# A router's first expert layer: three blocks of tokens by 15 part products, with the operands' sums moved between engines

## The chip, the cores and the metric

The kernel runs on one core of one Trainium2 chip. The metric is the device time of one execution in microseconds (us). Its engines are TensorE (PE, with PEld for its weight loads), VectorE (DVE), ScalarE (ACT), GpSimd (POOL) and SyncE (SP, which here only issues transfers). All data is float32.

## The reference, cut to what matters

A gated linear attention makes 3072 tokens of 384 values; a cosine router sends each token to one of eight experts, and the expert's two layers make the output.

```python
state = alpha_t * state + k_t (x) v_t;  y_t = q_t @ state      # 4 batches, 8 heads, 768 steps, 48 values a head
x = y as 3072 tokens x 384
xn = x / (norm(x) + 1e-6);  en = expert_emb / (norm(expert_emb) + 1e-6)
logits = xn @ en.T / tau                                        # 8 experts
expert_idx = argmax(logits);  gate = softmax(logits)[expert_idx]
for e in range(8):                                              # w1: 384 x 1024, w2: 1024 x 384
    h = relu(x[expert_idx == e] @ w1[e])
    out[expert_idx == e] = gate * (h @ w2[e])
```

## The kernel before, in words

The attention runs until about 155 us and nothing in it changes. Tokens are sorted by expert in DRAM as they are routed. Then `run(i)` goes over the eight experts. An expert has three blocks of 128 tokens (`NC`); of expert 0 two were done before (`EARLY`), and its single block takes the plain `first_layer`. What is more than three blocks of an expert goes through `half_block` of 64 rows, behind a branch in `run_extra`; in the profiled execution it ran three times. The weights of expert i + 2 are fetched while expert i runs.

**First layer of three blocks** (`first_layer_pair`, matmuls at L999). Hidden units are taken in four pairs of 128-wide tiles (f and f + 4). For each pair the 2 x 3 tiles of w1 and the tokens, in two halves of 192, are multiplied in the manner of Strassen: 11 products of 192 columns in place of 12, in four PSUM banks (`pq0` to `pq3`). Their left sides are tiles of w1 or the sums s1 to s4 and `dif` (`w1_m`), the right sides tokens or the sums t1 to t4 (`xT_m`). ScalarE copies a bank out (L1010) and does the ReLU (L1007); VectorE adds (`add`, by `by_dve`, so recorded at L922).

**Sums of the operands.** `mix_first(i + 1)` makes the next expert's five sums of w1 (128x512) and four of tokens (128x192) on VectorE (L976), after the first layer of expert i. `mix_weights` makes four sums of w2 as eight operations of 128x384 on GpSimd (L946), at the start of the expert that uses them. `mix_hidden` makes four sums of the hidden values on VectorE, in two parts, put as `fill` between the adds of the last two pairs and behind them.

**Second layer.** The third block goes through `second_layer`: eight matmuls of 384 columns (L906), evicted by VectorE with the gate (L909). Blocks 0 and 1 go through `second_layer_pair`: seven products of four matmuls of 192 columns (L1047), in four banks. ScalarE writes u0, u1 (L1061, L1062) and half of y0 (L1069), and VectorE collects the rest (`gated`, L1054). GpSimd scatters each block's output to its token rows with an indirect DMA (L817).

**Next expert's preparation.** `prepare` transposes a block of the next expert's tokens on TensorE (L842) after each pair of tiles, and VectorE copies it to xT. `prepare_gates` (L850 to L877) makes the next expert's gates: squares and square root on ScalarE (L857, L858), the largest logit and differences on VectorE (L870 to L873, `gsh`), Exp on ScalarE (L874), sum and reciprocal on VectorE.

**What sets the order.** Each engine runs its instructions in one order, which a scheduler sets when the kernel is built; `turn_of` and `issue_after` fix parts of it. TensorE's products follow the list `pe`, and VectorE's adds the list `dve`; `done_pair` holds the last work of a pair, behind which the next expert's branch and GpSimd's sums stand. Between two experts all engines read the branch's condition (L1165).

```python
def by_dve(call, *args):
    with turn_of(dve):
        dve[:] = [call(*args)]
    return dve[0]
...
hT = hp.tile([P, FT, NC * P], FP32, name="hT")[:, :, 0:n]
```

Of the kernel before, what the change touches and what calls it, by code (L numbers as in the profile page):

```python
# [27 lines left out]
def kernel(  # L28
# [756 lines left out]
    with ExitStack() as c3:  # L785
# [15 lines left out]
        w1_m = wp.tile([P, 5, F // 2], FP32, name="w1_m")  # L801
        xT_m = xp.tile([P, 4, NC * P // 2], FP32, name="xT_m")
# [34 lines left out]
        def turn(xg, xT, n, by=None):  # L837

            px = ps_x.tile([P, KT, P], FP32, name="pxg")
            with turn_of(pe if by else []):  # L840
                for k in range(KT):
                    done = nc.tensor.transpose(  # L842
                        px[:, k, 0:n], xg[0:n, k * P : (k + 1) * P], ident[0:n, 0:n]
                    )
            if by is None:
                return nc.vector.tensor_copy(xT, px[:, :, 0:n])
            pe[:] = [done]
            return by(nc.vector.tensor_copy, xT, px[:, :, 0:n])
# [51 lines left out]
        def second_layer(w2_t, hT, gate, col):  # L900

            py = ps_y.tile([P, DM], FP32, name="pyo")
            y = yp.tile([P, DM], FP32, name="y")
            with pe_turn():
                for f in range(FT):
                    pe[:] = [nc.tensor.matmul(  # L906
                        py, lhsT=hT[:, f], rhs=w2_t[:, f], start=(f == 0), stop=(f == FT - 1),
                    )]
            nc.vector.tensor_scalar(y, py, gate, None, ALU.mult)  # L909
            with turn_of(drained):  # L910
                return scatter(y, col)
# [6 lines left out]
        fill = []  # L918
# [5 lines left out]

        def filled(n):
            for _ in range(min(n, len(fill))):
                fill.pop(0)()
# [8 lines left out]
        def mix_weights(w2_t, j):  # L936
# [3 lines left out]
            to, x, y = ((t1, b12, b11), (t2, b22, t1), (t4, b21, t2), (t3, b22, b12))[j]  # L940

            n = FT // 4
            with turn_of(done_pair):
                for k in range(2):
                    f = slice(k * n, k * n + n)
                    nc.gpsimd.tensor_tensor(to[:, f], x[:, f], y[:, f], ALU.subtract)  # L946

        def mix_hidden(hT, f0, f1):

            a11, a12, a21, a22 = (  # L950
                hT[:, j * FT // 2 + f0 : j * FT // 2 + f1, i * P : i * P + P]
                for i in range(2) for j in range(2)
            )
            s1, s2, s3, s4 = (hT_m[:, k, f0:f1] for k in range(4))
            for to, x, y, op in (
                (s1, a21, a22, ALU.add), (s2, s1, a11, ALU.subtract),
                (s4, a12, s2, ALU.subtract), (s3, a11, a21, ALU.subtract),
            ):
                yield lambda to=to, x=x, y=y, op=op: by_dve(nc.vector.tensor_tensor, to, x, y, op)

        def mix_first(i):

            w1_t, xT = w1_s[i % NW], xT_s[i % 2]
            a11, a12, a21, a22 = quarters_w1(w1_t, 0, F // 2)
            m = NC * P // 2
            (b11, b12), (b21, b22) = ((xT[:, k, 0:m], xT[:, k, m : 2 * m]) for k in range(2))
            s1, s2, s3, s4, dif = (w1_m[:, k] for k in range(5))
            t1, t2, t3, t4 = (xT_m[:, k] for k in range(4))
            for to, x, y, op in (
                (s1, a21, a22, ALU.add), (s2, s1, a11, ALU.subtract),  # L970
                (s3, a11, a21, ALU.subtract), (s4, a12, s2, ALU.subtract),
                (dif, w1_t[:, 2, 0 : F // 2], w1_t[:, 2, F // 2 : F], ALU.subtract),
                (t1, b12, b11, ALU.subtract), (t2, b22, t1, ALU.subtract),
                (t3, b22, b12, ALU.subtract), (t4, b21, t2, ALU.subtract),
            ):
                nc.vector.tensor_tensor(to, x, y, op)  # L976

        def quarters_w1(w1_t, c0, c1):
            return [w1_t[:, k, j * F // 2 + c0 : j * F // 2 + c1] for j in range(2) for k in range(2)]

        def first_layer_pair(w1_t, hT, xT, f):

            cut = slice(f * P, f * P + P)
            a11, a12, a21, a22 = quarters_w1(w1_t, f * P, f * P + P)
            m = NC * P // 2
            r1, r2 = slice(0, m), slice(m, 2 * m)
            s1, s2, s3, s4, dif = (w1_m[:, k, cut] for k in range(5))  # L990
            t1, t2, t3, t4 = (xT_m[:, k] for k in range(4))
            c1, c2 = w1_t[:, 2, cut], w1_t[:, 2, F // 2 + f * P : F // 2 + f * P + P]
            a, b, c, d = (bank(j)[:, 0:m] for j in range(4))
            u1, u2, u3 = (yp.tile([P, m], FP32, name=f"v{j}", bufs=2) for j in range(3))
            h1, h2 = hT[:, f], hT[:, FT // 2 + f]

            def product(to, left, right, start, stop):
                with pe_turn():
                    pe[:] = [nc.tensor.matmul(  # L999
                        to, lhsT=left, rhs=right, start=start, stop=stop, skip_group_check=True,  # L1000
                    )]

            def add(to, p, u):
                by_dve(nc.vector.tensor_tensor, to, p, u, ALU.add)

            def relu(h, p):
                return nc.scalar.activation(h, p, AF.Relu)  # L1007

            product(a, a11, xT[:, 0, r1], True, False)
            nc.scalar.copy(u1, a)  # L1010
            product(b, s2, t2, True, True)
            add(u2, b, u1)
            product(c, s3, t3, True, False)
            add(u3, c, u2)
            filled(1)
            product(d, c2, xT[:, 2, r2], True, False)
            product(d, s1, t1, False, False)
            add(h2[:, r2], d, u3)
            filled(1)
            product(a, a12, xT[:, 1, r1], False, False)  # L1020
            product(a, c1, xT[:, 2, r1], False, True)
            relu(h1[:, r1], a)
            product(c, a22, t4, False, False)
            product(c, c2, xT[:, 2, r1], False, True)
            add(h2[:, r1], c, u2)
            relu(h2, h2)
            product(d, s4, xT[:, 1, r2], False, False)
            product(d, dif, xT[:, 2, r2], False, True)
            add(h1[:, r2], d, u2)
            filled(2)  # L1030
            return relu(h1[:, r2], h1[:, r2])
        def second_layer_pair(w2_t, hT, gate, col):
# [5 lines left out]
            a11, a12, a22 = hT[:, 0:n, 0:P], hT[:, n:FT, 0:P], hT[:, n:FT, P : 2 * P]  # L1038
            a, b, c, d = (bank(j)[:, 0:m] for j in range(4))
            y0 = yp.tile([P, DM], FP32, name="y")  # L1040
            y1 = yp.tile([P, DM], FP32, name="y")
            g0, g1 = gate[:, 0:1], gate[:, 1:2]
# [15 lines left out]

            u = yp.tile([P, 5, m], FP32, name="u", bufs=1)
            product(a, a11, b11, True, False)  # L1060
            nc.scalar.mul(u[:, 0], a, g0)  # L1061
            nc.scalar.mul(u[:, 1], a, g1)  # L1062
            product(b, s2, t2, True, True)
            gated(u[:, 2], b, g0, u[:, 0])
            gated(u[:, 3], b, g1, u[:, 1])
            product(c, s3, t3, True, False)
            gated(u[:, 4], c, g1, u[:, 3])
            product(a, a12, b21, False, True)
            nc.scalar.mul(y0[:, 0:m], a, g0)  # L1069
            product(d, s1, t1, True, False)  # L1070
            gated(y1[:, m:DM], d, g1, u[:, 4])
            product(c, a22, t4, False, True)
            gated(y1[:, 0:m], c, g1, u[:, 3])
            scatter(y1, col[:, 1:2])
            product(d, s4, b22, False, True)
            done_pair[:] = pe[0], gated(y0[:, m:DM], d, g0, u[:, 2])
            done_pair.append(scatter(y0, col[:, 0:1]))
# [33 lines left out]
        def run(i):  # L1111
# [5 lines left out]
            hT = hp.tile([P, FT, NC * P], FP32, name="hT")[:, :, 0:n]  # L1117
            pair = blocks_run(i) == NC
            dve[:] = [] if pair else ready
            if pair:  # L1120
                for j in range(4):
                    mix_weights(w2_t, j)
                for f in range(FT // 2):
                    done = first_layer_pair(w1_t, hT, xT, f)
                    if f < len(nxt):
                        turned = prepare(i + 1, f, by_dve)

                    if f >= FT // 4:
                        f0 = 2 * (f - FT // 4)
                        fill.extend(mix_hidden(hT, f0, f0 + 2))  # L1130
                filled(len(fill))
# [5 lines left out]
            if nxt:  # L1137
                with turn_of(dve):
                    mix_first(i + 1)
# [8 lines left out]
            for t in range(2 if pair else 0, blocks_run(i)):  # L1148
                sent = second_layer(
                    w2_t, hT[:, :, t * P : (t + 1) * P], gate[:, t : t + 1], col[:, t : t + 1]  # L1150
# [67 lines left out]
        gates(exg[:, 0:EARLY], egt[:, 0:EARLY], esx[:, 0:EARLY], EARLY)  # L1218
# [8 lines left out]

        for i in range(E):
# [37 lines left out]
```

## Time and profile before

| | |
|---|---|
| three runs | 417.14, 415.33, 417.24 us, median 417.14 |
| profiled execution | 415.06 us; span from first to last instruction 413.3 us |
| granted TensorE clock, mean | 0.994 |
| VectorE, ScalarE, GpSimd busy | 267.8, 178.4, 190.9 us |
| first layer, products of three blocks (L999) | 280 passes on plain tiles, 168 on two sums, and smaller groups |
| VectorE's adds of a bank into hidden values (L922) | 84 of 128x192, 357 ns each |
| GpSimd's w2 sums (L946) | 56 of 128x384, 998 and 996 ns each |

An execution of the program is recorded by the hardware profiler; the page gives each engine's busy time, the chain of work that ended last, and groups of instructions with count, busy time and mean length. A timeline row reads: start in us, length in us, engine, line of the code, operation, output <- inputs, shape, and how many instructions in a row it holds; in brackets the idle time ahead and what ended it. Matmuls are pipelined, so rows that follow each other overlap a little; the pace is read from start to start. One fp32 matmul is two passes of the array, and each pass has a record of its own.

### The profile page before, as it was taken

The numbers are of one execution on the slowest core, as the hardware profiler recorded it, in microseconds if no ns is written. First come the engines' busy times: TensorE is split into PE (matmuls) and PEld (weight loads), VectorE is DVE, ScalarE is ACT, GpSimd is POOL, SyncE is SP. The second block draws the span as 40 slices with busy tenths as digits, with TensorE's granted clock in tenths as the row PEclk, the third lists the DMA queues.
The fourth block names the chain that finished last, engine by engine and source line by source line (L and its number), as shares of the span: only waits on it lengthen the run. The fifth ranks groups of instructions, "written<-read, shape, count | busy, mean of one in ns | idle before, by whom it ended". The sixth has DMA issues, their size and how long they took to land. (4 is left out here: it accounts for less than half of the span.)

```text
span 413.3 us, 11425 instructions
## 1 busy us (share of the span) xinstructions
PE 403.6 (98%) x4346; PEld 358.6 (87%) x4346; DVE 267.8 (65%) x725; ACT 178.4 (43%) x430; POOL 190.9 (46%) x283
## 2 busy tenths in 40 slices
PE   6999999999999999999999999999999999999994
PEld 6888999899889886879799799799989979979974
DVE  6899788788898334715855845943672694593541
ACT  4555554555455435453523523522451352452410
POOL 7446787777766547308018028024301802702701
PEclk9999999999999999999999999999999999999999
DMA  9999999999998944959009219117303801001001
GB/s 137 160 162 157 159 214 172 199 182 205 194 185 257 387 172 143 293 186 365 6 18 321 92 39 329 56 38 272 121 19 105 302 2 38 22 0 53 3 17 43
DMA packets 119374, 60.20 MB, mean 146 GB/s; under 512 B 102287, under 2 KB 113816, under 8 KB 119312
## 3 DMA queue, kind: packets, MB, share of 16 engines
q1 hardware_dynamic: 115208, 49.14, 51.0%
q0 software_dynamic: 3728, 10.16, 7.1%
q8 instruction: 41, 0.67, 0.8%
q14 instruction: 21, 0.17, 0.1%
q10 hardware_dynamic: 376, 0.05, 0.1%
HBM read 49.69 MB, written 11.45 MB: 148 GB/s over the span
## 5 line engine op out<-in xcount | busy, mean ns | idle before, releaser
L817 POOL DMA_INDIRECT out_dram<-y,sx x25 | 24.4, 977 | 158.1 <-DVE gsh L873 77.6
L999 PE MATMUL pq<-xT,w 128*128 128x192 f32 x280 | 64.5, 328 | 0.6
L922 DVE TENSOR_TENSOR hT<-pq,v 128x192 f32<-128x192 f32 x84 | 30.0, 357 | 32.8 <-PE pq L999 30.8
L999 PEld LDWEIGHTS pq<-xT,w 128*128 128x128 f32 x280 | 47.3, 190 | 2.8 <-DVEq L1165 1.7
L507 POOL TENSOR_TENSOR qs<-qc,a 128x512 f32<-128x512 f32 x24 | 30.6, 1275 | 33.9 <-DVE a L503 23.4
L906 PE MATMUL pyo<-w,hT 128*128 128x384 f32 x128 | 43.3, 492 | 0.0
L906 PEld LDWEIGHTS pyo<-w,hT 128*128 128x128 f32 x128 | 23.7, 190 | 15.3
L999 PE MATMUL pq<-xT_m,w_m 128*128 128x192 f32 x168 | 36.5, 326 | 0.0
L1007 ACT ACTIVATE hT<-hT 128x384 f32<-128x384 f32 (+1 forms) x56 | 24.8, 443 | 23.1 <-DVE hT L922 19.9
L479 DVE TENSOR_TENSOR_SCAN r<-pa,inr 128x511 f32<-128x511 f32 x24 | 29.2, 1216 | 6.3 <-PE pa L194 4.4
L503 DVE TENSOR_TENSOR_SCAN a<-pa,ini 128x512 f32<-128x512 f32 x24 | 29.3, 1223 | 1.1
L1047 PE MATMUL pq<-w_m,hT_m 128*128 128x192 f32 x168 | 29.6, 326 | 0.0
L946 POOL TENSOR_TENSOR w_m<-w 128x384 f32<-128x384 f32 x28 | 27.4, 998 | 3.5 <-DMA out_dram<-y,sx 2.7
L999 PEld LDWEIGHTS pq<-xT_m,w_m 128*128 128x128 f32 x168 | 28.9, 190 | 0.0
L313 POOL DMA_INDIRECT xs<-x,dest x24 | 24.3, 1012 | 9.5 <-issue 4.5
L1007 ACT ACTIVATE hT<-pq 128x192 f32<-128x192 f32 x28 | 9.2, 330 | 43.5 <-PE pq L999 43.5
L1047 PEld LDWEIGHTS pq<-w_m,hT_m 128*128 128x128 f32 x168 | 27.7, 190 | 0.0
L946 POOL TENSOR_TENSOR w_m<-w,w_m 128x384 f32<-128x384 f32 x28 | 27.1, 996 | 0.0
L191 PE MATMUL sc<-qs,kr 64*64 64x128 f32 x768 | 26.5, 276 | 0.0
L191 PE MATMUL pyx<-sm,vt 128*64 128x128 f32 x384 | 26.3, 279 | 0.0
L922 DVE TENSOR_TENSOR v<-pq,v 128x192 f32<-128x192 f32 x56 | 20.0, 356 | 9.1 <-ACT v L1010 4.4
L1054 DVE SCALAR_TENSOR_TENSOR y<-pq,gt,u 128x192 f32<-128x192 f32 x21 | 8.8, 418 | 24.6 <-PE pq L1047 24.6
(199 smaller groups left out, 896.5 us busy)
## 6 DMA issues: line engine op xcount, KB each, us to landing
w<-in_moe_w_dram SPq DMA_DIRECT2D x16, 1536.0 KB, 9.2
kt<-in_k_dram SPq DMA_DIRECT2D x24, 192.0 KB, 4.3
qt<-in_q_dram SPq DMA_DIRECT2D x24, 192.0 KB, 4.5
vt<-in_v_dram SPq DMA_DIRECT2D x24, 192.0 KB, 5.8
xg<-xs SPq DMA_DIRECT2D x22, 196.5 KB, 7.7
at<-in_alpha_dram SPq DMA_DIRECT2D x24, 168.0 KB, 5.0
xg<-xs SPq DMA_DIRECT2D x8, 98.2 KB
at<-in_alpha_dram SPq DMA_DIRECT2D x24, 22.5 KB, 4.2
```

The source lines that it names most:

```text
L191: last["pe"] = nc.tensor.matmul(*args, **kwargs)
L313: ins = nc.gpsimd.indirect_dma_start(out=xs, out_offset=bass.IndirectOffsetOnAxis(ap=rows, axis=0), in_=x, in_offset=None, bounds_check=E ...
L479: nc.vector.tensor_tensor_scan(r[:, L - 2 :: -1], pa[:, L - 1 : 0 : -1], inr[:, L - 2 :: -1], 1.0, ALU.mult, ALU.add,)
L503: d["a_scan"] = by_dve = nc.vector.tensor_tensor_scan(a, pa, ini, 0.0, ALU.mult, ALU.add)
L507: by_pool = nc.gpsimd.tensor_tensor(qs.rearrange("p n t -> p (n t)"), d["qc"], a, ALU.mult)
L817: ins = nc.gpsimd.indirect_dma_start(out=out, out_offset=bass.IndirectOffsetOnAxis(ap=col, axis=0), in_=y, in_offset=None, bounds_check=N - 1,
L906: pe[:] = [nc.tensor.matmul(py, lhsT=hT[:, f], rhs=w2_t[:, f], start=(f == 0), stop=(f == FT - 1),)]
L922: dve[:] = [call(*args)]
L946: nc.gpsimd.tensor_tensor(to[:, f], x[:, f], y[:, f], ALU.subtract)
L999: pe[:] = [nc.tensor.matmul(to, lhsT=left, rhs=right, start=start, stop=stop, skip_group_check=True,)]
L1007: return nc.scalar.activation(h, p, AF.Relu)
L1047: pe[:] = [nc.tensor.matmul(to, lhsT=left[:, f], rhs=right[:, f], start=start and f == 0, stop=stop and f == n - 1, skip_group_check=True,)]
```

## The change

The first layer now takes an expert's three blocks at once (`first_layer_blocks`): a product's left side is four tiles of w1 side by side or of its sums (128x512), its right side one block of 128 tokens or a sum of blocks; 15 products of four matmuls make the 2 x 3 outputs, each of 128x512 in one bank. A bank is read on its way (copied by ScalarE or added by VectorE into the hidden values in place) and accumulated on by later products. `between` puts the next expert's transposes after products 3, 6, 9 and 14, and ScalarE copies them. There are ten sums of w1, made by GpSimd one expert ahead (those of expert 1 by VectorE, after the gates of the blocks that were done early), and the sums of blocks by VectorE, in 13 operations of 128x128 or 128x256. The four sums of w2 move to VectorE, as four operations of 128x768. The hidden sums are four operations of 128x512 after the first layer. The third block's output is evicted by ScalarE. The pair's second layer collects s-products and a22's in bank a, which is read by ScalarE or VectorE and accumulated on four times; y0 is scattered before y1. The hidden values have one buffer in place of two.

In the order that the scheduler sets, ScalarE's u0 (L1093 after) stands behind the Exp of the next expert's gates (L872 after), where u0 and u1 stood ahead of it; and VectorE's w2 sums for an expert stand in the second layer of the expert before it, t1 and t2 ahead of the gated y1, t3 and t4 behind it and on either side of the last gated y0.

Removed functions are in the code above; of the new ones all lines are shown.

```diff
-        w1_m = wp.tile([P, 5, F // 2], FP32, name="w1_m")
-        xT_m = xp.tile([P, 4, NC * P // 2], FP32, name="xT_m")
+        w1_m = wp.tile([P, 10, F // 2], FP32, name="w1_m")
+        xT_m = xp.tile([P, 16, P], FP32, name="xT_m")
...
-            return by(nc.vector.tensor_copy, xT, px[:, :, 0:n])
+            return by(xT, px[:, :, 0:n])
...
-            nc.vector.tensor_scalar(y, py, gate, None, ALU.mult)
+            by(y, py, gate)
...
-        def mix_weights(w2_t, j):
+        def mix_weights(w2_t):
             (b11, b12), (b21, b22) = quarters(w2_t)
             t1, t2, t3, t4 = (w2_m[:, k] for k in range(4))
-            to, x, y = ((t1, b12, b11), (t2, b22, t1), (t4, b21, t2), (t3, b22, b12))[j]
...
-                    nc.gpsimd.tensor_tensor(to[:, f], x[:, f], y[:, f], ALU.subtract)
+            for to, x, y in ((t1, b12, b11), (t2, b22, t1), (t3, b22, b12), (t4, b21, t2)):
+                by_dve(nc.vector.tensor_tensor, to, x, y, ALU.subtract)
...
+        def hidden(hT, t):
+            return [hT[:, j * FT // 2 : (j + 1) * FT // 2, t * P : (t + 1) * P] for j in range(2)]
+        def mix_hidden(hT):
+            (a11, a12), (a21, a22) = (hidden(hT, t) for t in range(2))
+            s1, s2, s3, s4 = (hT_m[:, k] for k in range(4))
             for to, x, y, op in (
+                (s3, a11, a21, ALU.subtract), (s1, a21, a22, ALU.add),
+                (s2, s1, a11, ALU.subtract), (s4, a12, s2, ALU.subtract),
             ):
+                by_dve(nc.vector.tensor_tensor, to, x, y, op)
...
+        def mix_first_weights(i, by):
+            (a11, a12, a13), (a21, a22, a23) = halves_w1(w1_s[i % NW])
+            g, g2, e, f2, q9, q7, q10, k6, q13, k = (w1_m[:, j] for j in range(10))
             for to, x, y, op in (
+                (g, a11, a12, ALU.add), (g2, g, a22, ALU.subtract), (e, a12, a13, ALU.subtract),
+                (f2, e, a22, ALU.subtract), (q9, a21, g2, ALU.subtract),
+                (q7, a23, q9, ALU.subtract), (q10, g, q7, ALU.subtract),
+                (k, f2, a23, ALU.add), (k6, k, a21, ALU.subtract),
+                (q13, q7, a13, ALU.subtract),
             ):
+                by(to, x, y, op)
...
+        def mix_first_rows(i):
+            xT, m = xT_s[i % 2], xT_m
+            b1, b2, b3 = (xT[:, k, 0 : NC * P].rearrange("p (t n) -> p t n", n=P) for k in range(KT))
+            y1, z1, y2, z2, x5, x12, x10, x6, x1, x4, x7, x13, s, x15, x11, x14 = (
+                m[:, j : j + 1] for j in range(16)
+            )
+            v = nc.vector
+            def one(b, t):
+                return b[:, t : t + 1]
+            v.tensor_tensor(m[:, 0:2], b2[:, 1:3], b3[:, 1:3], ALU.add)
+            v.tensor_tensor(y2, one(b2, 0), one(b1, 0), ALU.subtract)
+            v.tensor_tensor(x1, y1, y2, ALU.add)
+            v.tensor_tensor(x11, y2, one(b3, 0), ALU.add)
+            v.tensor_tensor(m[:, 4:6], b1[:, 0:2], y1.to_broadcast([P, 2, P]), ALU.subtract)
+            v.scalar_tensor_tensor(
+                out=x4, in0=y2, scalar=-1.0, in1=one(b3, 1), op0=ALU.mult, op1=ALU.subtract
+            )
+            v.tensor_tensor(x7, z1, one(b1, 0), ALU.subtract)
+            v.tensor_tensor(s, one(b2, 2), one(b3, 1), ALU.add)
+            v.tensor_tensor(m[:, 6:8], s.to_broadcast([P, 2, P]), b1[:, 0:3:2], ALU.subtract)
+            v.tensor_tensor(x13, one(b1, 2), z1, ALU.subtract)
+            v.tensor_tensor(z2, one(b1, 2), one(b2, 2), ALU.subtract)
+            v.tensor_tensor(x14, one(b3, 0), x7, ALU.subtract)
+            v.tensor_tensor(x15, one(b1, 1), x6, ALU.add)
...
+        def first_layer_blocks(w1_t, hT, between):
+            (a11, a12, a13), (a21, a22, a23) = halves_w1(w1_t)
+            g, g2, e, f2, q9, q7, q10, k6, q13, k = (w1_m[:, j] for j in range(10))
+            y1, z1, y2, z2, x5, x12, x10, x6, x1, x4, x7, x13, _, x15, x11, x14 = (
+                xT_m[:, j] for j in range(16)
+            )
+            (c11, c21), (c12, c22), (c13, c23) = (hidden(hT, t) for t in range(NC))
+            n = FT // 2
+            def grid(j):
+                return bank(j)[:, 0 : n * P].rearrange("p (f t) -> p f t", t=P)
+            A, B, C, D = (grid(j) for j in (2, 1, 3, 0))
             def product(to, left, right, start, stop):
                 with pe_turn():
+                    for f in range(n):
+                        pe[:] = [nc.tensor.matmul(
+                            to[:, f], lhsT=left[:, f * P : (f + 1) * P], rhs=right,
+                            start=start and f == 0, stop=stop, skip_group_check=True,
+                        )]
+            def add(c, p):
+                by_dve(nc.vector.tensor_tensor, c, p, c, ALU.add)
+            def relu(c, p):
+                return nc.scalar.activation(c, p, AF.Relu)
+            product(A, a22, x1, True, False)
+            nc.scalar.copy(c21, A)
+            product(B, g2, y1, True, False)
+            nc.scalar.copy(c12, B)
+            product(D, a13, x11, True, True)
+            nc.scalar.copy(c11, D)
+            between()
+            product(A, f2, y2, False, False)
+            add(c11, A)
+            product(B, g, x5, False, False)
+            add(c11, B)
+            relu(c11, c11)
+            D = grid(0)
+            product(D, a11, x12, True, True)
+            add(c12, D)
+            between()
+            product(A, e, x4, False, False)
+            add(c12, A)
+            relu(c12, c12)
+            product(B, q7, x7, False, False)
+            nc.scalar.copy(c13, B)
+            product(C, q10, x10, True, False)
+            nc.scalar.copy(c23, C)
+            between()
+            product(A, k6, x6, False, False)
+            add(c13, A)
+            product(B, q9, z1, False, False)
+            add(c23, B)
+            product(C, q13, x13, False, True)
+            add(c13, C)
+            relu(c13, c13)
+            product(A, k, z2, False, False)
+            add(c23, A)
+            relu(c23, c23)
+            product(B, a23, x14, False, True)
+            add(c21, B)
+            relu(c21, c21)
+            between()
+            product(A, a21, x15, False, True)
+            return relu(c22, A)
...
+            a, b, d = (bank(j)[:, 0:m] for j in (0, 1, 3))
+            u = yp.tile([P, 3, m], FP32, name="u", bufs=1)
...
             product(a, a11, b11, True, False)
             nc.scalar.mul(u[:, 0], a, g0)
-            nc.scalar.mul(u[:, 1], a, g1)
-            product(b, s2, t2, True, True)
-            gated(u[:, 2], b, g0, u[:, 0])
-            gated(u[:, 3], b, g1, u[:, 1])
-            product(c, s3, t3, True, False)
-            gated(u[:, 4], c, g1, u[:, 3])
-            product(a, a12, b21, False, True)
-            nc.scalar.mul(y0[:, 0:m], a, g0)
+            product(b, a12, b21, True, True)
+            gated(y0[:, 0:m], b, g0, u[:, 0])
+            product(a, s2, t2, False, False)
+            nc.scalar.mul(u[:, 1], a, g0)
             product(d, s1, t1, True, False)
-            gated(y1[:, m:DM], d, g1, u[:, 4])
-            product(c, a22, t4, False, True)
-            gated(y1[:, 0:m], c, g1, u[:, 3])
-            scatter(y1, col[:, 1:2])
+            nc.scalar.mul(u[:, 2], d, g1)
+            product(a, s3, t3, False, False)
+            gated(y1[:, m:DM], a, g1, u[:, 2])
             product(d, s4, b22, False, True)
-            done_pair[:] = pe[0], gated(y0[:, m:DM], d, g0, u[:, 2])
-            done_pair.append(scatter(y0, col[:, 0:1]))
+            gated(y0[:, m:DM], d, g0, u[:, 1])
+            scatter(y0, col[:, 0:1])
+            product(a, a22, t4, False, True)
+            done_pair[:] = pe[0], nc.scalar.mul(y1[:, 0:m], a, g1)
+            done_pair.append(scatter(y1, col[:, 1:2]))
...
-            hT = hp.tile([P, FT, NC * P], FP32, name="hT")[:, :, 0:n]
+            hT = hp.tile([P, FT, NC * P], FP32, name="hT", bufs=1)[:, :, 0:n]
...
             if pair:
-                for j in range(4):
-                    mix_weights(w2_t, j)
-                for f in range(FT // 2):
-                    done = first_layer_pair(w1_t, hT, xT, f)
-                    if f < len(nxt):
-                        turned = prepare(i + 1, f, by_dve)
-                    if f >= FT // 4:
-                        f0 = 2 * (f - FT // 4)
-                        fill.extend(mix_hidden(hT, f0, f0 + 2))
-                filled(len(fill))
+                mix_weights(w2_t)
+                left = list(range(len(nxt)))
+                rest = []
+                def between():
+                    if left:
+                        rest[:] = [prepare(i + 1, left.pop(0), nc.scalar.copy)]
+                done = first_layer_blocks(w1_t, hT, between)
+                if nxt:
+                    turned = rest[0]
+                mix_hidden(hT)
...
             if nxt:
+                if pair:
+                    mix_first_weights(i + 1, nc.gpsimd.tensor_tensor)
                 with turn_of(dve):
-                    mix_first(i + 1)
+                    mix_first_rows(i + 1)
...
                 sent = second_layer(
-                    w2_t, hT[:, :, t * P : (t + 1) * P], gate[:, t : t + 1], col[:, t : t + 1]
+                    w2_t, hT[:, :, t * P : (t + 1) * P], gate[:, t : t + 1], col[:, t : t + 1],
+                    nc.scalar.mul if pair else nc.vector.tensor_scalar_mul,
                 )
...
-        gates(exg[:, 0:EARLY], egt[:, 0:EARLY], esx[:, 0:EARLY], EARLY)
+        known = gates(exg[:, 0:EARLY], egt[:, 0:EARLY], esx[:, 0:EARLY], EARLY)
...
+        with turn_of([known]):
+            mix_first_weights(1, nc.vector.tensor_tensor)
```

## The prediction

> **What bounds the kernel now.** I read the busy table, then the chain that ended last, then TensorE's timeline for one expert, and at last what the other engines do in that expert's second half.
>
> ```profile
> PE 403.6 (98%) x4346; PEld 358.6 (87%) x4346; DVE 267.8 (65%) x725; ACT 178.4 (43%) x430; POOL 190.9 (46%) x283
> ...
> PE 7%; POOL 0%; issue 0%; POOLq 0%; DVE 0%
> PE pq L999 3%; PE pq L1047 2%; PE pyo L906 1%; POOL out_dram L817 0%; POOLq L1161 0%; DVE y L1054 0%
> ```
>
> TensorE is busy for 98% of the span, and the chain ends in its products: the first layer (L999), the second layer of the pair (L1047) and of the third block (L906). VectorE has a third of its time free and GpSimd half. So fewer TensorE passes are worth their whole time, and work on VectorE, ScalarE or GpSimd costs nothing until TensorE must wait for it. TensorE waits for them at few places, so one late result shows at once.
>
> **The gain on TensorE.** An expert's first layer is now 4 x 11 products; each is one fp32 matmul, which the trace records as two passes, so 88 passes of 192 columns. After, it is 15 x 4 matmuls, 120 passes of 128 columns. The timeline of TensorE has rows for both widths:
>
> ```profile
> 167.93 1.50 PE L894 MATMUL pq<-xT,w 128*128 128x128 f32 x12
> 169.27 0.49 PE L842 MATMUL pxg<-ident,xg 128*128 128x128 f32 x3
> ...
> 303.45 1.46 PE L1047 MATMUL pq<-w,hT 128*128 128x192 f32 x8
> 304.75 2.76 PE L1047 MATMUL pq<-w_m,hT_m 128*128 128x192 f32 x16
> ```
>
> From start to start, eight passes of 192 columns take 1.30 us (162.5 ns each), and twelve of 128, each with weights of its own, take 1.34 us (111.7 ns each). So 88 x 162.4 ns = 14.29 us becomes 120 x 111.7 ns = 13.40 us: 0.89 us less, times the seven experts with three blocks = **-6.2 us**. The columns fall by an eleventh (15,360 for 16,896), and a column of the narrow pass costs 0.873 ns for 0.846; the gain is what is left. The second layer keeps its 16 + 56 passes.
>
> The Trainium skill ("TensorE: Matmul & The Clock Gate", Back-to-back issue gap) speaks against narrow products: 81 ns for a matmul of 128 columns and 131 ns for one of 512, much more per column. By an estimate from that page, a straight line between the two, 192 columns take 89 ns, and the change would cost TensorE some 13 us over the seven experts in place of saving 6. The rows above do not agree (111.7 and 162.4 ns), and they decide.
>
> **Handovers inside the first layer.** A bank is written by a product, read by ScalarE (copy of 128x512, 0.59 us at L489) or VectorE (add with one operand in PSUM, 0.69 us at L486), and accumulated on three products later. A product takes 8 x 0.1117 = 0.89 us, so two products, 1.79 us, lie between; the way out of TensorE is some 0.3 us (a pass's latency and its semaphore), so bank and reader need about 1.0 us. Slack 0.6 us or more; only the last product has less, and in the last expert, without a transpose in front of it, I charge **+0.2 us** once. The gap of 0.3 us at the branch between experts stays. Copies of xT go to ScalarE, which is busy for 43%: nothing.
>
> **The start.** Expert 1's ten w1 sums go to VectorE, 10 x 0.60 us = 6.0 us where 5 x 0.60 + 1.3 were. They may stand in front of a copy of xT near 172.6 us. Between nothing (VectorE's free third) and 1.2 us (two such sums), I take **+0.5 us**.
>
> **w2's sums on VectorE.** Four of 128x768, about 0.95 us each (estimate from 0.68 for 512 and 0.42 for 256 columns), during the second layer. They stand in VectorE's queue ahead of the gated y1 (L1088), which the last product waits for, since it accumulates in the same bank. From the end of the fourth product the queue needs t1 + t2 + y1 = 0.95 + 0.95 + 0.42 + 0.4 of latency = 2.7 us, and the fifth and sixth products cover 2.6. I take 0.15 us each, x 6 = **+0.9 us** (bounds 0 and 0.4 each).
>
> **One bank for the collection.** Before, product 3 of the pair writes a bank of its own. After, it accumulates into bank a, so it must wait until ScalarE's u0 (L1093) has read a. In ScalarE's queue u0 stands behind the Exp of the next expert's gates. Exp needs gsh, which VectorE computes after the hidden sums and row sums. The trace of before has the same chain, with u first:
>
> ```profile
> 304.95 0.42 ACT L1061 ACTIVATE u<-pq,gt 128x192 f32<-128x192 f32 x1 [2.27 <-PE pq L1047]
> 305.27 0.41 ACT L1062 ACTIVATE u<-pq,gt 128x192 f32<-128x192 f32 x1
> 305.70 1.28 ACT L874 ACT_TABLE_LOAD   x1
> 306.99 0.23 ACT L874 ACTIVATE gsh<-gsh 128x32 f32<-128x32 f32 x1
> ```
>
> Let T be the start of an expert's first layer and T1 its end, T + 15.0 (13.4, four groups of transposes of 0.33, the gap of 0.3 at the branch). Undisturbed, VectorE runs three dependent hidden sums from T1 + 1.2 (the last relu) at 0.71 each to T1 + 3.3, the row sums (three of 256, ten of 128 columns, 0.36 and 0.2 apart) to T1 + 6.3, and gsh by T1 + 6.85. ScalarE has squares (4 x 0.645), a table load 1.28, y2's product, the next table by T1 + 7.35, Exp to 7.6, u0 to 8.0. Product 3 would start at T1 + 5.26 (third block) + 2 x 1.30 less the load of its weights ahead, T1 + 7.70. So even undisturbed it waits about 0.36 us, six times: +2.2 us. This edit alone takes a third of the gain.
>
> **w1's sums on GpSimd.** Ten of 128x512 at 1.275 us (L507's row, same shape, two operands in SBUF) = 12.75 us. The fifth must wait for product 11 (T + 11.3), which reads the old q9, so q10 runs to about T1 + 0.3, and k, q13 and k6 follow to T1 + 4.05: beside VectorE's hidden sums, whose two operands both lie in SBUF. Before's GpSimd sums (L946) fell at the start of a first layer, where VectorE's adds have one operand in PSUM (0.36 us beside them and without). What two SBUF operands do beside a GpSimd sum, the attention part shows. VectorE first, then GpSimd:
>
> ```profile
> 9.73 0.98 DVE L293 TENSOR_TENSOR en<-en,rtau 8x1 f32<-8x1 f32 x1
> ...
> 92.43 0.60 DVE L334 TENSOR_TENSOR win<-x,top 128x16 f32<-128x16 f32 x1
> 93.07 0.17 DVE L335 TENSOR_TENSOR win<-win,first 128x16 f32<-128x16 f32 x1
> ...
> 105.07 0.48 DVE L334 TENSOR_TENSOR win<-x,top 128x16 f32<-128x16 f32 x1
> ```
>
> ```profile
> 9.43 1.26 POOL L507 TENSOR_TENSOR qs<-qc,a 128x512 f32<-128x512 f32 x1 [1.73 <-DVE al L282]
> ...
> 92.39 0.61 POOL L532 TENSOR_TENSOR dec<-state,end 128x256 f32<-128x256 f32 x1
> 92.95 0.19 POOL L775 COPY x<-toks 128x2 f32<-128x2 f32 x1
> ...
> 104.89 0.61 POOL L532 TENSOR_TENSOR dec<-state,end 128x256 f32<-128x256 f32 x1
> ```
>
> An operation of one column takes 0.98 us and ends when GpSimd's does (9.73 + 0.98 = 10.71; 9.43 + 1.26 = 10.69). The two at L334 end at 93.03 and 105.55, GpSimd's at 93.00 and 105.50; alone the like takes 0.17 to 0.19. So the VectorE operation stands still until the running GpSimd sum is done. Where the two take turns, each hidden sum meets one more GpSimd sum: s1 waits about 1.0 us for k, then s2 and s4 wait 1.275 each for q13 and k6; 3.5 us in all. Where GpSimd runs on through, VectorE starts at its end, T1 + 4.05, with s3 still to do, so s1 starts at T1 + 4.65 in place of 1.2: 3.45 us. I take 3.5. The bounds are 0 (VectorE goes first and GpSimd waits, which costs nothing: its sums are due 11 us later, at T + 30) and 4.45 (from T + 14.6 to T1 + 4.05).
>
> The Trainium skill ("SBUF — State Buffer", Who interferes with whom) says the same against this change: a VectorE instruction with two SBUF inputs contends with a GpSimd instruction that reads SBUF, and the one that issues second is blocked for all of the other. It names no price; by its rule alone either engine may lose, and by the rows VectorE did.
>
> 0.5 us of the 3.5 is covered, since the table load ends 0.5 us after gsh was due. Product 3 waits 0.36 + 3.0 = 3.36 us, six times (the last expert prepares no gates): **+20.2 us** in place of 2.2.
>
> **Sum.** -6.2 + 0.2 + 0.5 + 0.9 + 20.2 = +15.6 us on the profiled execution's 415.06 us: 430.7. That execution lies 2.1 us under the median of the three runs, 417.14; the change is added to the median: **432.7 us**. A difference under 0.5%, 2.1 us, can't be told from none.
>
> **Rivals.**
> - *No collision*: VectorE gets its operands first, or GpSimd is done earlier. Then product 3 waits 0.36 and the sum is -6.2 + 0.2 + 0.5 + 0.9 + 2.2 = -2.4: 414.7 us, faster. It decides from a VectorE delay of 0.9 us: there 6 x 0.76 us and the other terms eat the 6.2. One GpSimd sum in the way (1.275 us) is already over it. For it: GpSimd's due time is far off. Against it: the rows above, where VectorE waited each time.
> - *Half a collision*: once VectorE has the operands it keeps them through its back-to-back sums, and only s3 and s1 wait: about 1.9 us, product 3 waits 1.76, sum +6: 423 us. For it: at 92.95 GpSimd had another instruction ready, and VectorE still finished.
> - *Collision, and a slower TensorE after each pause*: before has no pause of 3 us in the experts and its mean granted clock is 0.994, so no row here prices it. The clock's records have one stretch of 3.41 us at half speed, at the sparse start; one such stretch after each pause costs 1.7 us, six times +10: 443 us.
> - *Full gain*: u0 and y1 are never late: -6.2 + 0.2: 411 us.
> - *The change doesn't do what it says*: GpSimd's ten sums would have to be later than the next first layer, T + 30; they end near T + 19. I give it nothing.
>
> **Chances.** The forecast 0.47, no collision 0.17, half a collision 0.15, the slower clock 0.12, full gain 0.09. Full gain and two thirds of no collision are faster by over 0.5%: 0.20; the rest of it and a little of the half collision are the same: 0.08; slower 0.72. The range leaves out the full gain and most of the slower clock: 413 to 440 us.
>
> **What would show it.** TensorE's passes of the new first layer (L1013) 112 ns apart, 13.4 us for a first layer. GpSimd rows at L965 of 1.28 us, the last four after T1. Hidden sums (L919, 128x512) of over 1 us that end with a GpSimd row. A gap in TensorE of some 3.4 us ahead of the third product of the pair, ended by ScalarE's L1093, which stands behind Exp (L872). If the hidden sums take 0.7 us beside GpSimd's, the forecast is wrong and the first rival holds; if they are long and the gap is missing, the wait for u0 was misjudged.

## The result, and the profile after

The changed kernel takes 434.52 us (median of four runs, 432.65 to 436.2), the kernel before 416.94 us; the ratio is 1.0431 (95% interval 1.0387 to 1.0475). The forecast was 432.7 us, in a range of 413 to 440. The profiled execution of the changed kernel took 436.2 us with a span of 434.1 us, 20.8 us more than the span before.

From the page of the changed kernel, the busy table, the granted clock and two groups:

```profile
PE 403.9 (93%) x4570; PEld 358.8 (83%) x4570; DVE 283.8 (65%) x634; ACT 196.9 (45%) x433; POOL 221.3 (51%) x287
...
PEclk9999999999999999999999999899989996999999
...
L1081 PE MATMUL pq<-w_m,hT_m 128*128 128x192 f32 x168 | 35.2, 376 | 16.5 <-ACT u L1093 16.5
...
L965 POOL TENSOR_TENSOR w_m<-w_m,w 128x512 f32<-128x512 f32 x30 | 41.6, 1393 | 1.4
```

TensorE fell from 98% busy to 93%. Its largest idle time, 16.5 us, stands ahead of the pair's products, and it was ended by ScalarE's u0 (L1093). Three slices of the clock's row are under 9, where before none was. The timeline of TensorE, from the end of one first layer to the next:

```profile
207.31 2.76 PE L1081 MATMUL pq<-w,hT 128*128 128x192 f32 x16
212.93 4.17 PE L1081 MATMUL pq<-w_m,hT_m 128*128 128x192 f32 x24 [2.86 <-ACT u L1093]
216.94 1.46 PE L1081 MATMUL pq<-w,hT_m 128*128 128x192 f32 x8
...
219.58 0.83 PE L1013 MATMUL pq<-xT_m,w 128*128 128x128 f32 x6
222.31 0.46 PE L1013 MATMUL pq<-xT_m,w 128*128 128x128 f32 x2 [1.89 <-PEq L1199]
...
227.72 2.84 PE L1013 MATMUL pq<-xT_m,w_m 128*128 128x128 f32 x24
230.40 0.49 PE L842 MATMUL pxg<-ident,xg 128*128 128x128 f32 x3
```

The first two products (16 passes) run, then TensorE stands for 2.86 us ahead of the third. The new passes do what was expected of them: 24 from 227.72 to 230.40, 111.7 ns each. The pause of 1.89 us at the branch was not foreseen. ScalarE's timeline in the same stretch shows who was late:

```profile
208.11 1.28 ACT L872 ACT_TABLE_LOAD   x1
212.34 0.23 ACT L872 ACTIVATE gsh<-gsh 128x32 f32<-128x32 f32 x1 [2.95 <-DVE gsh L871]
212.48 0.40 ACT L1093 ACTIVATE u<-pq,gt 128x192 f32<-128x192 f32 x1
```

The table was there at 209.4; Exp then waited 2.95 us for VectorE's gsh, and u0 behind it. What held VectorE, seen one expert later in its timeline, and GpSimd's beside it:

```profile
236.01 1.29 DVE L919 TENSOR_TENSOR hT_m<-hT 128x512 f32<-128x512 f32 x1
...
237.31 1.14 DVE L862 TENSOR_TENSOR xg<-xg,used 128x4 f32<-128x4 f32 x1
...
238.49 1.23 DVE L863 TENSOR_SCALAR none<-xg 128x4 f32<-128x4 f32 x1
...
239.82 1.76 DVE L919 TENSOR_TENSOR hT_m<-hT 128x512 f32<-128x512 f32 x1
241.62 0.69 DVE L919 TENSOR_TENSOR hT_m<-hT_m,hT 128x512 f32<-128x512 f32 x1
```

```profile
235.47 1.28 POOL L965 TENSOR_TENSOR w_m<-w_m 128x512 f32<-128x512 f32 x1
236.70 4.34 POOL L965 TENSOR_TENSOR w_m<-w_m,w 128x512 f32<-128x512 f32 x3
```

Four VectorE operations, two of them of four columns, take over 1.1 us each while GpSimd's last four sums run; the one that starts after GpSimd's end (241.04) takes 0.69.

Where the 20.8 us lie, from the start of each stretch to the start of the next in TensorE's two timelines:

| stretch | before, us | after, us | difference |
|---|---|---|---|
| first layers of experts 1 to 7, with the gap at the branch | 110.73 | 105.67 | -5.1 |
| third blocks and expert 0's block | 42.02 | 41.30 | -0.7 |
| pair's second layer, experts 1 to 6 | 9.10 each | 12.27, 12.27, 13.78, 13.91, 15.22, 11.56 | +24.4 |
| pair's second layer, expert 7 | 9.26 | 9.26 | 0 |
| three half blocks | 16.65 | 18.25 | +1.6 |
| ahead of the experts and behind the last pass | 180.01 | 180.60 | +0.6 |

Of the 24.4, 5 x 3.17 + 2.46 = 18.3 us are the wait. The other 6.1 are what 13.78, 13.91 and 15.22 have over 12.27: there the clock's records have stretches of half speed, 3.41, 3.41 and 6.83 us long, that begin between 0.7 us before and 1.3 us after the pause's end. The longest one lies over the 24 passes behind expert 5's pause, which take 7.15 us where 4.17 are usual:

```profile
358.65 7.15 PE L1081 MATMUL pq<-w_m,hT_m 128*128 128x192 f32 x24 [2.87 <-ACT u L1093]
```

### The profile page after: what moved, and what is told of

It reads as the page before. It is cut to its first block, busy times and chain, and to the rows that moved or that the text cites. A ratio compares the mean times of both kernels' runs of the same rounds, so it can differ in the third digit from the quotient of the medians.

```text
span 434.1 us, 11748 instructions
## 1 busy us (share of the span) xinstructions
PE 403.9 (93%) x4570; PEld 358.8 (83%) x4570; DVE 283.8 (65%) x634; ACT 196.9 (45%) x433; POOL 221.3 (51%) x287
## 5 line engine op out<-in xcount | busy, mean ns | idle before, releaser
L919 DVE TENSOR_TENSOR hT<-pq,hT 128x512 f32<-128x512 f32 x63 | 43.5, 691 | 51.1 <-PE pq L1013 49.4
L1013 PE MATMUL pq<-xT_m,w_m 128*128 128x128 f32 x560 | 67.2, 275 | 0.0
L1013 PEld LDWEIGHTS pq<-xT_m,w_m 128*128 128x128 f32 x560 | 64.7, 192 | 0.3 <-issue 0.3
L1081 PE MATMUL pq<-w_m,hT_m 128*128 128x192 f32 x168 | 35.2, 376 | 16.5 <-ACT u L1093 16.5
L1081 PEld LDWEIGHTS pq<-w_m,hT_m 128*128 128x128 f32 x168 | 33.3, 225 | 18.2 <-ACT u L1093 18.2
L965 POOL TENSOR_TENSOR w_m<-w_m,w 128x512 f32<-128x512 f32 x30 | 41.6, 1393 | 1.4
L1022 ACT ACTIVATE hT<-hT 128x512 f32<-128x512 f32 x35 | 22.1, 631 | 42.7 <-DVE hT L919 42.3
L1013 PE MATMUL pq<-xT_m,w 128*128 128x128 f32 x280 | 38.4, 277 | 2.3 <-PEq L1199 1.9
L1013 PEld LDWEIGHTS pq<-xT_m,w 128*128 128x128 f32 x280 | 34.9, 192 | 3.9 <-issue 3.5
L904 PEld LDWEIGHTS pyo<-w,hT 128*128 128x128 f32 x128 | 23.7, 190 | 14.8
L965 POOL TENSOR_TENSOR w_m<-w 128x512 f32<-128x512 f32 x12 | 15.3, 1273 | 17.6 <-PE pq L1013 17.6
L191 PEld LDWEIGHTS sc<-qs,kr 64*64 64x64 f32 x768 | 20.7, 133 | 4.0 <-issue 3.0
L191 PEld LDWEIGHTS pyx<-sm,vt 128*64 128x64 f32 x384 | 20.5, 136 | 4.1 <-issue 4.0
```

What stands on the lines that cost most here:

```text
L191: last["pe"] = nc.tensor.matmul(*args, **kwargs)
L904: pe[:] = [nc.tensor.matmul(py, lhsT=hT[:, f], rhs=w2_t[:, f], start=(f == 0), stop=(f == FT - 1),)]
L965: by(to, x, y, op)
L1013: pe[:] = [nc.tensor.matmul(to[:, f], lhsT=left[:, f * P : (f + 1) * P], rhs=right, start=start and f == 0, stop=stop, skip_group_check=Tr ...
L1022: return nc.scalar.activation(c, p, AF.Relu)
L1081: pe[:] = [nc.tensor.matmul(to, lhsT=left[:, f], rhs=right[:, f], start=start and f == 0, stop=stop and f == n - 1, skip_group_check=True,)]
```

## The experiments

The theory: GpSimd's w1 sums hold up VectorE's operations with two operands in SBUF, so gsh, Exp, u0 and with it the third product are late. The rivals: ScalarE's own queue makes u0 late; the amount of work moved does it, not its coincidence; the collision hurts TensorE by other ways too. Each kernel is compared with the kernel before on its own chip: the runs c, e, g2 and h were on one where that takes 424.70 us, those of a, b, d and g on one with 416.07, the last three on one with 416.89.

**a: no sums on GpSimd.**

```diff
-                if pair:
-                    mix_first_weights(i + 1, nc.gpsimd.tensor_tensor)
```

> Leaves out GpSimd's ten sums of w1 for experts 2 to 7 (their products use expert 1's sums, so the output is another). Theory (VectorE stands behind GpSimd's sums, and u0 behind VectorE by way of Exp): hidden sums beside nothing take 0.69 us, the pause ahead of the pair's third product falls from 2.9 us to 0.4 or less, the half-clock stretches go, 414 us (412 to 416). Rival (u0 is late because of ScalarE's own queue, squares and two table loads): the pause stays over 2 us and the time over 428.

Measured 411.94 us, ratio 0.9903 (0.9879 to 0.9927). VectorE's timeline:

```profile
201.33 0.68 DVE L919 TENSOR_TENSOR hT_m<-hT 128x512 f32<-128x512 f32 x1
...
202.03 0.15 DVE L862 TENSOR_TENSOR xg<-xg,used 128x4 f32<-128x4 f32 x1
...
202.25 0.16 DVE L863 TENSOR_SCALAR none<-xg 128x4 f32<-128x4 f32 x1
...
202.60 0.69 DVE L919 TENSOR_TENSOR hT_m<-hT 128x512 f32<-128x512 f32 x1
```

The same four operations take 0.68, 0.15, 0.16 and 0.69 us, and each second layer of a pair 9.33 in place of 12.27 to 15.22. ScalarE's queue by itself costs 0.23 us an expert: its rival falls.

**b: Exp behind u2.** The last steps of the next expert's gates are kept in a list and issued after the pair's last use of bank d.

```diff
-            nc.scalar.activation(sh, sh, AF.Exp)
...
+            def tail():
+                nc.scalar.activation(sh, sh, AF.Exp)
...
+            kept = gated(y0[:, m:DM], d, g0, u[:, 1])
+            for tail in later:
+                with turn_of([u2, kept]):
+                    tail()
```

> Exp of the next expert's gates and what follows it are issued after the pair's u2; GpSimd's sums and the collection in one bank stay. Theory: the collision stays (VectorE's first hidden sum 1.3 us, small gate operations over 1 us), but nothing that TensorE waits for stands behind it: pause ahead of the third product gone, 412 us (410 to 415). Rival (VectorE's delay reaches TensorE by another way, the hidden sums s2 and s1 or the gated y1): a pause of 1.5 us or more per expert stays ahead of another product, 422 or more.

Measured 411.34 us, ratio 0.9890 (0.9872 to 0.9908). TensorE's timeline, and a line of VectorE's:

```profile
206.60 2.76 PE L1088 MATMUL pq<-w,hT 128*128 128x192 f32 x16
209.20 4.06 PE L1088 MATMUL pq<-w_m,hT_m 128*128 128x192 f32 x24
213.10 1.46 PE L1088 MATMUL pq<-w,hT_m 128*128 128x192 f32 x8
214.40 1.50 PE L1088 MATMUL pq<-w_m,hT 128*128 128x192 f32 x8
```

```profile
204.84 1.77 DVE L926 TENSOR_TENSOR hT_m<-hT 128x512 f32<-128x512 f32 x1
```

VectorE is held up as before (1.77 us), and no product of the pair waits: the third starts 2.60 us after the first. So the collision by itself is not the cost; it became one through ScalarE's order and the bank that u0 must free. The first layer, the two moves of the sums and the one bank all stay in this kernel, and it is faster than the one before.

**d: the pair collected in four banks again.** The old products and five u's, the rest as changed.

```diff
-            a, b, d = (bank(j)[:, 0:m] for j in (0, 1, 3))
+            a, b, c, d = (bank(j)[:, 0:m] for j in range(4))
```

> The pair's second layer is collected as before the change, in four banks with five u's; all else as changed. Theory: u0 and u1 are as late as in the changed kernel, but they are needed only by the fourth product, two products later than now: the pause is 0.7 us there in place of 3, no half-clock stretch, 420 us (417 to 423). Rival (the collision itself holds TensorE, whatever the banks): 430 or more.

Measured 423.30 us, ratio 1.0181 (1.0146 to 1.0215), a little over the expectation's range. TensorE's timeline:

```profile
207.95 2.76 PE L1080 MATMUL pq<-w_m,hT_m 128*128 128x192 f32 x16
212.59 1.57 PE L1080 MATMUL pq<-w,hT 128*128 128x192 f32 x8 [1.88 <-ACT u L1094]
```

The pause moves to the fourth product and is 1.88 us. I had counted two products of cover; it is one: 2.86 - 1.30 + 0.31 for u1, which must be read too, is 1.87. So with the same collision, one bank against four is worth about 1 us an expert in this order (3.17 against 2.15 us over 9.10, where no stretch of half clock is). The other 2.15 us stay when u0 and u1 have the old banks and stand behind Exp.

**g and g2: TensorE kept busy in the pause.** Nine unused matmuls ahead of the third product; g has them in all experts, g2 not in the last.

```diff
+            w = bank(2)[:, 0:m]
+            with pe_turn():
+                for f in range(9 if more else 0):
+                    pe[:] = [nc.tensor.matmul(
+                        w, lhsT=a12[:, f % n], rhs=b21[:, f % n],
+                        start=f == 0, stop=f == 8, skip_group_check=True,
+                    )]
             product(a, s2, t2, False, False)
```

> Nine matmuls of 192 columns that nothing uses (18 passes, 2.9 us) are put into a free bank ahead of the pair's third product, so TensorE isn't idle while u0 is late. Theory that the pauses themselves bring the stretches of half clock: none is left, each second layer of the pair takes 12.3 to 12.5 us, 430 us (428 to 432), less than the changed kernel although there is more work. Rival (the clock falls for another reason): stretches stay and the time is that of the changed kernel or more, 434 to 438.

> The nine unused matmuls ahead of the pair's third product again, now not in the last expert, which has no pause to fill and paid 2.9 us for them. Theory that the pauses bring the stretches of half clock: each second layer of the pair takes 12.3 us, none of them 13.8 to 15.2, 431 us (429.5 to 432.5). Rival (the stretches cost nothing on the median, or come from elsewhere): 434 or more.

g: 434.27 us, ratio 1.0437 (1.0411 to 1.0464), no better than the changed kernel. My number had left out that the last expert pays 2.93 us for matmuls with no pause to fill, and expert 6 0.5; and a stretch of half clock came all the same, behind a pause of 2.33 us at a branch. g2: 436.17 us, 11.5 us over the kernel before on its chip (the 431 that I expected were 14 over), ratio 1.0272 (1.0235 to 1.0308), where the changed kernel is 17.6 and 19.1 us over on others. The clock's row in its page:

```profile
PEclk9999999999999999999999999999999999999999
```

Each second layer of the pair takes 12.1 to 12.3 us in g2, none 13.8 or more: with TensorE busy, half clock does not come. That the stretches belong to the pauses is shown. What they are worth on the median is not settled: by g2 some 6 to 8 us against the changed kernel's distance on the other chips, by g, whose 18.2 us less 3.4 for matmuls with no pause to fill are 14.8, and which still has one stretch, only some 3 to 4. The two profiled executions of the changed kernel have 6.1 us of them here and 8.1 in run j.

**c: the sums swapped back.** w2's on GpSimd at the start of an expert, w1's on VectorE behind the gates.

```diff
-                by_dve(nc.vector.tensor_tensor, to, x, y, ALU.subtract)
+                    nc.gpsimd.tensor_tensor(to[:, f], x[:, f], y[:, f], ALU.subtract)
...
-                    mix_first_weights(i + 1, nc.gpsimd.tensor_tensor)
+                    mix_first_weights(i + 1, lambda *a: sums.append(a))
```

> The sums are put back the other way round: w2's on GpSimd in eight operations of 128x384 at the start of an expert, w1's ten on VectorE behind the next expert's gates, between the gated y's; Exp stays ahead of u0. Theory (what costs is GpSimd's reading beside VectorE's two-operand sums, not the amount of either's work): hidden sums 0.69 us, the pair's second layer 9.3 to 9.5 us as without any w1 sums, 412 us (410 to 414). Rival (VectorE's added 6 us make y1 or the next first layer late): a new pause ahead of the seventh product or in the first layer, 417 or more.

Measured 422.27 us, 2.4 under the kernel before, ratio 0.9941 (0.9912 to 0.9970). The pair's second layers take 9.31 us each, as expected, though VectorE now makes ten sums of 0.68 us an expert in place of four of 0.95 and Exp still stands ahead of u0: VectorE's own work is not what costs. (GpSimd has less to do here; run e keeps its amount.) Of the 5 us that I expected half are missing. In the profiled execution expert 0's first layer ends some 4.5 us later than in e and g2 on the same chip:

```profile
174.81 2.63 PE L892 MATMUL pq<-xT,w 128*128 128x128 f32 x12 [2.07 <-DVE xT L844]
```

Here the first copies of xT stand behind expert 0's eviction (L907) in VectorE's queue, in e ahead of it. TensorE waits 2.07 us, later 0.89 us for another copy of xT, and a stretch of half clock of 3.41 us begins behind the first wait.

**e: GpSimd's last three sums behind its scatter.**

```diff
+            if pair and nxt:
+                with turn_of([sent]):
+                    mix_first_weights(i + 1, nc.gpsimd.tensor_tensor, slice(7, 10))
```

> All as changed, but GpSimd's last three w1 sums stand behind its scatter of the third block, so they start when VectorE's hidden sums and row sums are over. Theory: same work on every engine, but only q10 still meets VectorE, so u0 is late by no more than 0.4 us; the last three may meet w2's sums and make y1 up to 0.5 us late; 413 us (411 to 416). Rival (GpSimd's work costs by its amount, or u0 is late without a collision): 425 or more.

Measured 449.30 us, 24.6 over the kernel before, ratio 1.0589 (1.0539 to 1.0639): wrong by far. VectorE's timeline, then GpSimd's:

```profile
286.31 4.34 DVE L871 TENSOR_TENSOR gsh<-gsh,gsq 128x32 f32<-128x32 f32 x1
```

```profile
285.64 1.22 POOL L817 DMA_INDIRECT out_dram<-y,sx  x1 [5.88 <-ACT y L907]
286.89 3.70 POOL L965 TENSOR_TENSOR w_m<-w_m,w 128x512 f32<-128x512 f32 x3
```

The hidden and row sums ran free, but gsh, the one operation that Exp waits for, came just as GpSimd went on from its scatter to the sums: 32 columns took 4.34 us, from the scatter's last 0.6 us through all three sums. The pause ahead of the third product was 3.9 us:

```profile
291.27 5.78 PE L1081 MATMUL pq<-w_m,hT_m 128*128 128x192 f32 x24 [3.92 <-ACT u L1093]
```

The amount of GpSimd's work was the same as in the changed kernel; the place alone made it worse. That is the theory's mechanism at another operation, and my expectation of where it would strike was wrong.

**h: b, and expert 0's block evicted ahead of expert 1's gates.**

```diff
+                with turn_of([done, turned] + evicted):
+                    prepare_gates(i + 1)
```

> Exp behind u2 as in the run b_late_exp, and expert 0's block is evicted ahead of expert 1's gates, which wait for a fetch, so that the first half block need not wait for its bank. Theory: the pause of 0.4 to 1.4 us in the first half block goes, 410.8 us (409.5 to 411.8), about 1.2% under the kernel before the change. Rival (the pause moves to expert 1's first layer, where Exp now stands between ScalarE's copies): 411.5 or more.

Measured 419.50 us, 5.2 under the kernel before, ratio 0.9859 (0.9820 to 0.9898): no more than b's gain. The pause in the first half block is 0.26 us, and the rival's is there; ScalarE's timeline, then TensorE's:

```profile
194.18 1.28 ACT L874 ACT_TABLE_LOAD   x1
195.47 0.23 ACT L874 ACTIVATE gsh<-gsh 128x32 f32<-128x32 f32 x1
195.60 0.57 ACT L1035 COPY hT<-pq 128x512 f32<-128x512 f32 x1
```

```profile
196.22 1.16 PE L1021 MATMUL pq<-xT_m,w_m 128*128 128x128 f32 x8 [0.60 <-ACT hT L1035]
```

Exp with its table now stands ahead of the copy that frees a bank for the fifth product. The wait was moved.

**i, b2 and j: both cures, b again and the changed kernel again, on one chip.** i is c with b's order of Exp.

> Both cures at once: w2's sums on GpSimd and w1's on VectorE, so no two-operand sum meets GpSimd, and Exp behind u2, so u0 stands behind nothing. Theory: with the wait for u0 gone the collision costs nothing any more, so this is the same as Exp moved alone, within 1 us, some 4 to 5 us under the kernel before on the same chip. Rival (the collision costs TensorE in other places too, about 1 us an expert): 3 us or more under Exp moved alone.

> The kernel of b_late_exp once more, on the same chip as the run of both cures, to compare the two and to see whether its gain holds: 4 to 5.5 us under the kernel before.

> The changed kernel unaltered on the same chip, so that the cures stand beside it: 16 to 20 us over the kernel before, with one to four stretches of half clock, one or none behind each pause of 2.9 us, and a pause of 1.9 us or none at the branch ahead of expert 2.

j: 436.04 us, ratio 1.0451 (1.0406 to 1.0496), with six pauses of 2.15 to 2.87 us and four stretches of half clock. b2: 411.60 us, 0.9866 (0.9851 to 0.9881). i: 409.25 us, 0.9815 (0.9802 to 0.9828), the fastest of all. It lies 2.35 us under b2, between theory and rival. The pair's second layers differ little, 9.10 against 9.14 us; the profiled spans differ by 1.3 us, in expert 0 and the first half block; the rest I can't place.

## Why the prediction was right, and where its terms were off

- *The gain on TensorE*, -6.2 us: the row for 128 columns held (111.7 ns). Without the branch's 1.75 us the first layers gained 6.8 us. The gap of 0.3 us at the branch stays, as I had it: from start to start it is 0.31 us before and after.
- *The wait for u0*, the main step: right in mechanism and place. 3.36 us was forecast, and 0.15 for y1; together 3.17 us an expert were measured. Run b shows that u0's place behind Exp is needed for it, run a that GpSimd's sums are. The operations were not the ones I named: s1, s2 and s4 were to wait; in the trace s3, two operations of the gates and s1 did, and s2 and s4 came after GpSimd's end. The delay of gsh, 9.97 us after the first layer's end in the changed kernel against 6.34 in run a, is 3.6 us for the forecast's 3.5.
- *Undisturbed wait of 0.36 us and 0.15 for y1*: run a has 0.23 for both.
- *A slower TensorE after each pause* was given as a rival at 0.12, 1.7 us for each of six. It happened besides the forecast, in three of the six pauses of the profiled execution, one of them twice as long: 6.1 us. It should have been a term of the sum with its own chance.
- *The start*, 0.5 us: 1.6 us in the first half block and 0.24 ahead. I had looked at the copies of xT; what was late is the bank (a pause of 1.38 us that L907 ended). In VectorE's queue expert 0's eviction (L907) stood behind expert 1's gates, which waited for a fetch:

```profile
183.02 0.18 DVE L858 TENSOR_REDUCE gtop<-xg 128x4 f32<-128x32 f32 x1 [3.78 <-DMA xg<-xs]
...
183.63 0.61 DVE L907 TENSOR_SCALAR y<-pyo,gt 128x384 f32<-128x384 f32 x1
```

- *The branch*, nothing: one branch of the changed kernel cost 1.89 us. Pauses of 1.0 to 2.3 us at one branch are in ten of the twelve profiled executions with the new first layer (not in a and d). A packet of 16 KB of the instruction queue is on its way at or just ahead of each of them, but also at branches that cost 0.15 us, so that the engine waits for code there is a guess; the cause stays open.
- *The number*: the sum was 15.6 us, the profiled execution has 20.8, and the median, which the forecast met within 2 us, 17.6. On the profiled execution the terms left out or too small (half clock 6.1, branch 1.8, start 1.3) were partly made up by the wait (18.3 us in place of 20.2 and 0.9) and by 1.4 us more gained in first layers and third blocks. The path was right; that the number came so close is in part luck.

## What to carry to other kernels

Follow a late operation through the order of each queue to the first place where TensorE must have it: here two moves, a bank read before it is accumulated on (0.23 us an expert without GpSimd's sums, run a) and a sum on another engine (2.15 us with the old banks, run d), met in one operation that stood behind Exp (3.17 us), and moving Exp alone turned 4.3 to 4.5% slower into 1.1 to 1.3% faster. When work goes to GpSimd, list VectorE's operations with two SBUF operands that run at the same time, and its TENSOR_SCALAR, the smallest too. Then choose the time at which the sums run, not only the engine.

## What the runs showed of the hardware

- GpSimd's sums and VectorE's operations took turns in the changed kernel, yet in run e three GpSimd sums went by while one VectorE operation of 128x32 waited 4.34 us. A waiting operation isn't sure of the next turn. Nor does every one wait: the 128x32 TENSOR_TENSOR at L868, with two operands in SBUF, took 0.18 us between two that did.
- A TENSOR_SCALAR with one SBUF operand waits too: 1.23 us beside GpSimd's sum, 0.16 without. TENSOR_REDUCE does not (0.17 us beside the sums). The Trainium skill ("SBUF — State Buffer", Who interferes with whom) says that `tensor_scalar` can contend with GpSimd and that `tensor_reduce` never does on trn2, and the rows agree.
- Half clock came behind pauses as short as 1.9 us: in run d one of five pauses of 1.9 us was followed by a stretch of 3.41 us, in the changed kernel three of six pauses of up to 2.9 us, in run e all five of 3.9 us. Pauses for other reasons bring it too: one stretch of 3.41 us followed the branch's pause of 2.1 to 2.3 us in b2, g, h and i, none that of 2.1 and 2.2 us in c and g2. The Trainium skill ("TensorE: Matmul & The Clock Gate", HAM oscillation — how this bites in real kernels) speaks of gaps over some 3.4 us; the measurement says that shorter ones are enough at times.
